# A list scheduler inside the kernel sets the order of a fused windowed attention and MLP-mixer on one core

## The chip, the core and the metric

The kernel runs on one core of a Trainium2 chip. The core has five engines that work side by side: TensorE (PE, matrix products), VectorE (DVE), ScalarE (ACT), GpSimd (POOL) and SyncE (SP, which here only issues transfers), and 16 DMA engines that move data. Each engine works through its own instructions strictly in the order in which the program lists them, and waits where an operand is not ready. The metric is the device time of one execution in microseconds (us); lower is better.

## What is computed

Four batches, eight heads, 768 positions, head size 64; all in float32 in memory. `n_sink` is 4 and `window` is 128.

```python
scores = scale * np.matmul(q, k.transpose(0, 1, 3, 2))      # (4, 8, 768, 768)
keep = is_sink | in_window                                  # first 4 keys, or 0 <= i-j < 128
a = softmax(np.where(keep, scores, -1e9))
x = (a @ v) laid out as (4, 768, 512)                       # heads side by side
h = np.maximum(x.T @ w_tok1, 0) @ w_tok2                    # token mixing, 768 -> 256 -> 768
u = x + h.T
out = u + np.maximum(u @ w_ch1, 0) @ w_ch2                  # channel mixing, 512 -> 1536 -> 512
```

## The kernel before

The work comes in eight groups of four heads (two groups to a batch) and four mixers (one to a batch). Tiles have 128 rows.

**Attention of a group.** q, k and v come as float32 and are cast to bf16 (`cast`, `cast_all` and `cast_v`, on POOL, DVE or ACT). q and k are turned so that the head dimension lies on the partitions: groups 0 to 3 by transposes on PE with a copy out of PSUM (`tr`), groups 4 to 7 by DMA transposes that SP issues (`turn`, line 126). `sc(j, u)` multiplies for one pair of heads `j` and a third `u` of the keys, in PSUM tile `ps_s`; ACT takes the exponential of all of it in one instruction (`pT`, line 252). In groups 0 and 1 the mask is added on PE (`mneg`, line 240), later it is applied to `pT` by POOL (lines 256, 263, 266). `sk` does the four sink keys (`ks`, `ps_k`, `pk`). `pv(qt)` multiplies with v (`va`) and `vsink` for a tile of 128 queries into `ps_o`, and DVE divides by the sum (lines 296 and 297) into `x_b`.

**Mixer of a batch.** `tok1` (tile `ps_h`, four pieces of six products), `tok2` (`ps_u`, six pieces of two; DVE adds `x_b` at line 340, which gives `u_sb`), `utr` (turns `u_sb` into `uT`: on PE for batch 0, by DMA for the others, line 344), `ch1` (`ps_v`, 24 pieces of four products 384 wide; a ReLU into `v`, on ACT at line 357 for even pieces and on DVE at line 359 for odd ones), `ch2` (`ps_w`, six tiles of 12 products 512 wide, in three parts of four; DVE adds `u_sb` at line 369, SP stores).

**PSUM.** Three pools of two tiles each: `ps_sc` for the scores (two banks to a tile), `ps_mx` for `ps_h`, `ps_v`, `ps_w` (and `ps_u` of batch 0), `ps_ms` for the rest.

**Order.** It is written out by hand. Attention and token mixing of batch 0 come first, as a list (`seq`). Then, for each batch `b`, the list `main` of its channel mixing is walked, and the list `fill` (attention and token mixing of batch `b + 1`, loads, casts) is put in at fixed shares of `main`'s cost by `spread`. Loads of q, k and v are one transfer of 768 KB for a group of heads (384 KB for the first ones). The line that places the late setup work of batch 0 is this one:

```python
fill += [(0.15, build_mask0), (0.2, lambda: cast_sinks(GB, NG))]
```

`build_mask0` is two writes by DVE (lines 173 and 180) with two selects by POOL (lines 174 and 177) between them; `cast_sinks` writes `vsink` on DVE (lines 195 and 198).

Of the kernel before, what the change touches and what calls it, by code (L numbers as in the profile page):

```python
# [1 line left out]

# [7 lines left out]
FP32 = mybir.dt.float32  # L10
BF16 = mybir.dt.bfloat16
AF = mybir.ActivationFunctionType
ALU = mybir.AluOpType


@with_exitstack
def kernel(
# [43 lines left out]
    ident = singles.tile([P, P], BF16, name="ident")  # L61
    mask0 = singles.tile([P, 2, 2, P], BF16, name="mask0")
    mneg = singles.tile([P, 2, 2, 2, P], BF16, name="mneg")
    warm = singles.tile([P, 512], BF16, name="warm")
    ks = [[singles.tile([P, P], BF16, name=f"ks{a}{j}") for j in range(2)] for a in range(2)]
    dm = singles.tile([4 * GH, GH, 1], FP32, name="dm")
    vs_c = singles.tile([4 * GH, NG, D], FP32, name="vs_c")
    vsink = singles.tile([P, NG, GH, D1], BF16, name="vsink")

    w_tok1 = singles.tile([P, NT, DTOK], BF16, name="w_tok1")  # L70
    w_tok2 = singles.tile([P, NTOK, S], BF16, name="w_tok2")
    w_ch1 = singles.tile([P, NC, DCH], BF16, name="w_ch1")
    w_ch2 = singles.tile([P, NF, DM], BF16, name="w_ch2")

    SYNC = mybir.DependencyInfo(mybir.DependencyClass.Sync, mybir.DependencyReason.DATA)

    def after(dma, *others):
        for o in others:
            tc.add_manual_dep(dma.ins, o.ins.name, SYNC, reason="order of loads")
        return dma  # L80

    class Group:
        pass

    def tiles(g):
        G = Group()
        G.b, G.h0 = g // GB, GH * (g % GB)
        G.dma = g >= 2 * GB
        G.q32 = stage.tile([P, GH, NT, D], FP32, name="q32")
        G.k32 = stage.tile([P, GH, NT, D], FP32, name="k32")  # L90
        G.qb = bfp.tile([P, 2, NT, 2, D], BF16, name="qb")
        G.kb = bfp.tile([P, 2, NT, 2, D], BF16, name="kb")
        G.v32 = stage.tile([P, GH, NT, D], FP32, name="v32")
        G.va = bfp.tile([P, GH, NT, D1], BF16, name="va")
        G.T, G.pT = [None, None], [None, None]
        return G


    def load_qk(eng, src, dst, G, lo, hi):
        return eng.dma_start(  # L100
            out=dst[:, lo:hi].rearrange("p h t d -> p h (t d)"),
            in_=src[G.b, G.h0 + lo:G.h0 + hi].rearrange("h (p t) d -> p h (t d)", t=NT)
        ) if not G.dma else eng.dma_start(
            out=dst.rearrange("p h t d -> p (h t) d"),
            in_=src[G.b, G.h0:G.h0 + GH].rearrange("h (t p) d -> p (h t) d", p=P))

    def load_q(G, lo, hi, eng=nc.sync):
        return load_qk(eng, q, G.q32, G, lo, hi)

    def load_k(G, lo, hi, eng=nc.sync):  # L110
        return load_qk(eng, k, G.k32, G, lo, hi)

    def cast(G, j, which, copy):
        src, dst = ((G.q32, G.qb), (G.k32, G.kb))[which]
        copy(dst[:, j].rearrange("p t i d -> p i t d"), src[:, 2 * j:2 * j + 2])

    def flat(G, which):
        return (G.qb, G.kb)[which].rearrange("p j t i d -> p (j t i d)")

    def cast_all(G, which, copy):  # L120
        copy(flat(G, which).rearrange("p (t h d) -> p t h d", t=NT, h=GH),
             (G.q32, G.k32)[which].rearrange("p h t d -> p t h d"))

    def turn(G, which):
        T = att.tile([P, 2 * NT, P], BF16, name="qT" if which == 0 else "kT")
        nc.sync.dma_start_transpose(out=T, in_=flat(G, which))
        G.T[which] = [T.rearrange("d (t j) p -> d t j p", j=2)[:, :, j] for j in range(2)]

    def by_dve(o, i):
        nc.vector.tensor_copy(out=o, in_=i)  # L130

    def by_pool(o, i):
        nc.gpsimd.tensor_copy(out=o, in_=i)

    def by_act(o, i):
        nc.scalar.activation(o, i, AF.Copy)
# [466 lines left out]
```

## Time and profile before

| | us |
|---|---|
| median of three runs | 231.0 (229.96 to 231.47) |
| span of the profiled execution, first to last instruction | 229.2 |
| PE busy in it | 205.5 (90%) |
| DVE, ACT, POOL busy | 107.0, 90.5, 93.9 |
| mean granted TensorE clock | 0.993 |

The profiled execution has its span as its own time; no other time was taken of it. Busy time of PE counts a product until its modelled end, so short pauses between products hide in it. "Busy" shares are a mean over stages that have different limits, so the stages are read one by one. In the chain of the work that ended last, a row is a start, a length and what ran; "issue" is time in which an engine waited for nothing that the profile shows. In the rows of an engine's timeline the brackets at the end give the pause before the first instruction of the row and what ended it.

### The profile page before, as it was taken

The page shows a single profiled execution, that of the slowest core. Times are in us where ns is not written, and L with a number is a line of the kernel's source. Part 1 is how long each engine was busy: PE and PEld are TensorE (multiplying, and loading weights), DVE is VectorE, ACT ScalarE, POOL GpSimd, SP SyncE. Part 2 cuts the span into 40 slices and gives each one's busy share as a digit, 9 for nine tenths or more (in the row PEclk, how much of TensorE's full clock was granted, in tenths as well). Part 3 has the DMA queues.
Part 4 walks back from the last instruction along what each step waited for, and adds up shares of the span by engine and source line. Part 5 has one row for each costly group of instructions (what it writes and reads, how often), then busy time and mean ns, then how long its engine had stood idle before and what let it go on. Part 6 is the DMA issues. An engine that isn't in the chain of part 4 may idle for free.

```text
span 229.2 us, 3886 instructions
## 1 busy us (share of the span) xinstructions
PE 205.5 (90%) x1547; PEld 111.3 (49%) x1565; DVE 107.0 (47%) x241; ACT 90.5 (40%) x152; POOL 93.9 (41%) x123
## 2 busy tenths in 40 slices
PE   7898868499799999788899999987999999999993
PEld 2444734255355654344466644444566444554441
DVE  5674635826375547222364464324337463333331
ACT  2798144027976210287752200777542001311100
POOL 8659732501878991057397700266640000000000
PEclk9999999979999999999999999999999999999999
DMA  6999999999879934869999738790001055001122
GB/s 208 342 228 155 211 306 232 296 269 214 166 148 217 229 99 108 169 171 213 218 220 207 167 82 164 170 186 0 24 25 46 3 160 160 0 0 49 46 92 92
DMA packets 76353, 34.88 MB, mean 152 GB/s; under 512 B 66400, under 2 KB 72288, under 8 KB 76336
## 3 DMA queue, kind: packets, MB, share of 16 engines
q1 hardware_dynamic: 70384, 24.65, 50.4%
q0 software_dynamic: 4992, 8.69, 17.1%
q10 hardware_dynamic: 960, 1.31, 1.7%
q8 instruction: 12, 0.20, 0.4%
q14 instruction: 5, 0.04, 0.1%
HBM read 26.77 MB, written 6.29 MB: 144 GB/s over the span
## 4 chain that ended last, share of the span: by engine, by line
PE 58%; DMA 13%; ACT 11%; DVE 7%; issue 5%; POOL 3%; SPq 1%; POOLq 0%; DVEq 0%
PE ps_w L366 26%; PE ps_v L354 18%; ACT pT L252 7%; DMA w_ch<-in_moe_w_ch_dram 5%; DMA v<-in_v_dram 5%; PE ps_h L332 3%; PE ps_u L339 3%; PE ps_s L246 2%; ACT v L357 2%; DVE o L369 2%; DMA k<-in_k_dram 2%; DMA kT<-kb 2%; PE ps_o L284 2%; PE ps_o L288 1%; PE ps_o L279 1%
## 5 line engine op out<-in xcount | busy, mean ns | idle before, releaser
L354 PE MATMUL ps_v<-uT,w_ch 128*128 128x384 bf16 x384 | 75.4, 331 | 7.4 <-ACT v L357 3.0
L366 PE MATMUL ps_w<-w_ch,v 128*128 128x512 bf16 x275 | 68.0, 379 | 2.7 <-ACT v L357 1.9
L357 ACT ACTIVATE v<-ps_v 128x384 bf16<-128x384 f32 x48 | 23.8, 495 | 81.7 <-PE ps_v L354 44.9
L354 PEld LDWEIGHTS <-w_ch 128*128 128x128 bf16 x384 | 35.9, 99 | 37.7 <-issue 17.8
L359 DVE TENSOR_SCALAR v<-ps_v 128x384 bf16<-128x384 f32 x48 | 26.6, 554 | 45.9 <-PE ps_v L354 45.9
L252 ACT ACTIVATE pT<-ps_s 128x1024 bf16<-128x1024 f32 (+1 forms) x48 | 43.6, 959 | 9.0 <-PE ps_s L246 8.7
L366 PEld LDWEIGHTS <-v 128*128 128x128 bf16 x288 | 27.1, 98 | 32.2 <-issue 4.2
L256 POOL TENSOR_TENSOR pT<-pT,mask 128x512 bf16<-128x512 bf16 x12 | 13.8, 1153 | 47.0 <-ACT pT L252 47.0
L369 DVE TENSOR_TENSOR o<-ps_w,u_sb 128x512 f32<-128x512 f32 x24 | 16.6, 692 | 18.7 <-PE ps_w L366 18.6
L340 DVE TENSOR_TENSOR u_sb<-ps_u,x_b 128x512 bf16<-128x512 f32 x24 | 16.2, 688 | 19.3 <-PE ps_u L339 19.1
L263 POOL TENSOR_SCALAR_AFFINE_SELECT pT<-pT 128x640 bf16<-128x640 bf16 x24 | 18.3, 761 | 11.0 <-ACT pT L252 11.0
L297 DVE TENSOR_TENSOR x_b<-ps_o,rc 128x256 bf16<-128x256 f32 x42 | 17.8, 424 | 1.4
L296 DVE RECIPROCAL rc<-ps_o 128x4 f32<-128x4 f32 x42 | 7.4, 177 | 22.6 <-PE ps_o L288 12.2
L246 PE MATMUL ps_s<-qT,kT 64*128 64x256 bf16 x192 | 15.4, 264 | 2.9 <-DMA kT<-kb 1.2
L284 PE MATMUL ps_o<-va,pT 128*128 128x65 bf16 x192 | 16.4, 194 | 0.0
L284 PEld LDWEIGHTS <-pT 128*128 128x128 bf16 x192 | 14.1, 98 | 3.0 <-issue 0.4
L266 POOL TENSOR_SCALAR_AFFINE_SELECT pT<-pT 128x512 bf16<-128x512 bf16 x24 | 15.5, 647 | 0.0
L288 PE MATMUL ps_o<-va,pT 128*128 128x65 bf16 x160 | 14.9, 194 | 0.0
L332 PE MATMUL ps_h<-x_b,w_tok 128*128 128x256 bf16 x96 | 13.4, 272 | 1.0 <-DVE x_b L297 0.5
L339 PE MATMUL ps_u<-h,w_tok 128*128 128x512 bf16 x46 | 13.5, 379 | 0.7 <-DVE u_sb L340 0.3
L246 PEld LDWEIGHTS <-kT 64*128 64x128 bf16 x192 | 6.8, 94 | 14.1 <-issue 9.4
L334 ACT ACTIVATE h<-ps_h 128x256 bf16<-128x256 f32 x16 | 6.1, 383 | 18.8 <-PE ps_h L332 18.8
(63 smaller groups left out, 173.1 us busy)
## 6 DMA issues: line engine op xcount, KB each, us to landing
out_dram<-o SPq DMA_DIRECT2D x23, 256.0 KB, 2.2
v<-in_v_dram SPq DMA_DIRECT2D x6, 768.0 KB, 10.0
w_ch<-in_moe_w_ch_dram POOLq DMA_DIRECT2D x4, 768.0 KB, 14.1
q<-in_q_dram SPq DMA_DIRECT2D x4, 768.0 KB, 8.6
k<-in_k_dram SPq DMA_DIRECT2D x4, 768.0 KB, 10.4
q<-in_q_dram SPq DMA_DIRECT2D x4, 384.0 KB, 6.9
q<-in_q_dram POOLq DMA_DIRECT2D x2, 768.0 KB, 16.9
k<-in_k_dram POOLq DMA_DIRECT2D x2, 768.0 KB, 18.4
```

The costliest lines, as they stand in the source:

```text
L246: nc.tensor.matmul(ps[:, i, at:at + w].rearrange("p (c q) -> p c q", q=P), G.T[1][j][ds(64 * i, 64), kt], G.T[0][j][ds(64 * i, 64), kt:kt ...
L252: nc.scalar.activation(pT[:, :, 512 * u:512 * u + n], ps[:, :, 0:n], AF.Exp, scale=scale)
L263: nc.gpsimd.affine_select(out=cur, in_=cur, compare_op=ALU.is_ge, fill=0.0, base=0, pattern=[[0, NT - 1], [1, P]], channel_multiplier=-1)
L284: nc.tensor.matmul(o, pT[:, i, ds(256 * qt, P)], G.va[:, h, qt], start=(qt < 2 and h == 0), stop=(h == GH - 1 and qt == 0), skip_group_che ...
L297: nc.vector.tensor_tensor(out=x_b[:, qt, c0:c0 + GH * D].rearrange("p (h d) -> p h d", h=GH), in0=o[:, :, 0:D], in1=rc.to_broadcast([P, GH ...
L332: nc.tensor.matmul(ps, w_tok1[:, t, ts(tt, P)], x_b[:, t, ds(a * GH * D, GH * D)], start=(t == 0), stop=(t == NT - 1))
L339: nc.tensor.matmul(ps, w_tok2[:, tt, ts(st, P)], h1[:, tt], start=(tt == 0), stop=(tt == NTOK - 1))
L354: nc.tensor.matmul(ps, w_ch1[:, c, ts(ft, P)], uT[:, c, ds(half * HS, HS)], start=(c == 0), stop=(c == NC - 1))
L357: nc.scalar.activation(v1[:, ft, ds(half * HS, HS)], ps, AF.Relu)
L359: nc.vector.tensor_scalar(out=v1[:, ft, ds(half * HS, HS)], in0=ps, scalar1=0.0, scalar2=None, op0=ALU.max)
L366: nc.tensor.matmul(ps, v1[:, ft, ts(st, P)], w_ch2[:, ft], start=(ft == 0), stop=(ft == NF - 1))
L369: nc.vector.tensor_tensor(out=o, in0=ps, in1=u_sb[:, st], op=ALU.add)
```

## The change

All tiles are static (one allocation each, two or four copies with letters, `qTa`, `qTb`). The work is described as a list of tasks, each with engines that may run it, a duration, the tasks that it needs and a priority. A list scheduler (`Plan.order`) walks a clock and starts, on each free engine, the ready task with the lowest priority number; the tasks are then emitted in the order in which they started. The durations are formulas in the code; the hardware sees nothing of them but the order.

```diff
+class Plan:
+    LAT = {"PE": PE_TAIL + SEM, "ACT": 0.115 + SEM, "DVE": 0.093 + SEM, "POOL": 0.05 + SEM, "SP": 0.05}
...
+            for e in engines:
+                if free[e] > now + 1e-9:
+                    continue
...
+                    if len(t.eng) > 1:
+                        ends = {x: max(free[x], now) + self.cost(t, x) for x in t.eng}
+                        best = min(ends.values())
+                        if ends[e] > best + 0.12:
+                            held.append(item)
+                            continue
+                    if t.need:
+                        got = pick(t.need, now)
...
+def pe(*cols):
+    return sum(c / 2400 + 0.0025 for c in cols)
...
-    ps_sc = ctx.enter_context(tc.tile_pool(name="ps_sc", bufs=2, space=bass.MemoryType.PSUM))
-    ps_mx = ctx.enter_context(tc.tile_pool(name="ps_mx", bufs=2, space=bass.MemoryType.PSUM))
-    ps_ms = ctx.enter_context(tc.tile_pool(name="ps_ms", bufs=2, space=bass.MemoryType.PSUM))
+    ps_s = [psp.tile([P, 2, 512], FP32, name=f"ps_s{x}") for x in "ab"]
+    ps_g = [psp.tile([P, 512], FP32, name=f"ps_g{x}") for x in "abcd"]
...
+    CH = {"load": 0, "tr": 6, "sc": 7, "sk": 5, "pv": 4, "tok1": 3, "tok2": 2, "ut": 1}
...
+    l_ch1 = [load("POOL", w_ch1[:, :, ts(i, c1)], moe_w_ch1.rearrange("(t p) n -> p t n", p=P)[:, :, ts(i, c1)], 3.1,
+                  gate, prio=next(pp)) for i in range(N1)]
...
+        if G.dma:
+            for n, (src, dst, ld) in enumerate(((q, q32, "lq"), (k, k32, "lk"))):
+                setattr(G, ld, [load("SP", dst[s][:, h], rows_in_tiles(src, g, h, h + 1)[:, 0], 1.1, [*after_cast, *hold_back(b)],
+                                     prio=b * 10 + 8 + (g % GB), hold=0.95) for h in range(GH)])
...
+        size = 1 if g == 0 else 2
+        for n in range(0, 6, size):
+            todo = units[n:n + size]
...
+            m = add("PE", cost, f, [*[G.T[w][j] for w in range(2) for j in need], *([t_mneg] if first else [])],
+                    prio=pr(g, "sc"), need=("s", len(todo)), slot=slots)
...
+            M.v[half, ft] = add(("ACT", "DVE"), either(HS), e, [m, *(old.ch2[3 * half:3 * half + 3] if old else [])],
+                                prio=5, slot=slot, frees=True)
...
+                if b == B - 1 and st == NT - 1:
+                    ch2(st, 0, 256, False)
+                    ch2(st, 256, 128, False)
+                    ch2(st, 384, 128, True)
```

What this does to the program, part by part:

- **Four one-bank PSUM tiles** `ps_ga` to `ps_gd` serve everything but the scores, in any order; the two score tiles `ps_sa`, `ps_sb` stay. Scores after group 0 come in bursts of two units that take both score tiles at once.
- **Copies, ReLUs and casts** go to ACT or DVE (casts of the early groups also to POOL), whichever the plan sees free first.
- **The masks, the sink tiles and their writes** are made in the first microseconds.
- **Loads.** `w_ch1` comes in three pieces of 512 columns, `w_ch2` in two, all before q, k and v of group 2; v of groups 0 and 1 is issued by POOL and no longer by SP. q, k and v of groups 4 to 7 come one head at a time (192 KB).
- **POOL's masks** of groups 2 to 7 come in two pieces per pair of heads, the first after two of the three exponentials; before, they all came after the third.
- **The last output tile** is computed and stored in pieces of 256, 128 and 128 columns.

The instructions on PE are otherwise the same: 24 `ch1` pieces and six `ch2` tiles to a batch.

On DVE, around the first ReLUs of batch 0's channel mixing, the order before was (`u_sb` is the add of token mixing, `v_112` a ReLU):

```order
L340 TENSOR_TENSOR u_sb<-ps_u,x_b 128x512 x4
L359 TENSOR_SCALAR v_112<-ps_v 128x384
L340 TENSOR_TENSOR u_sb<-ps_u,x_b 128x512 x2
L173 MEMSET mask_92 128x512
L180 MEMSET mask_92 4x512
L359 TENSOR_SCALAR v_112<-ps_v 128x384
L195 TENSOR_SCALAR vsink<-vs_c,dm 16x6x64
L198 CAST vsink<-dm 16x6
```

In the change those writes of the mask stand among the first casts of the program (`kba` and `qba` are k and q of group 0 in bf16):

```order
L296 MEMSET mneg 4x128
L276 CAST kba<-k32a 128x2x6x64
L405 MEMSET mask_62 128x512
L276 CAST qba<-q32a 128x2x6x64
L407 MEMSET mask_62 4x512
L276 COPY qTa<-ps_gb 128x768
```

The mask has moved from between two ReLUs to the program's start, ahead of the copy of group 0's first turned q.

On ACT, at the start of batch 1's channel mixing, where group 4's attention begins, the order before was (`pT` an exponential of scores, `v_572` a ReLU of `ch1`, `ks` small copies of sink keys):

```order
L357 ACTIVATE v_572<-ps_v 128x384 x2
L229 ACTIVATE ks_95<-kT 64x4 x2
L229 ACTIVATE ks_96<-kT 64x4 x2
L252 ACTIVATE pT<-ps_s 128x2x512 x2
L357 ACTIVATE v_572<-ps_v 128x384
L252 ACTIVATE pT<-ps_s 128x2x384
L252 ACTIVATE pT<-ps_s 128x2x512
L357 ACTIVATE v_572<-ps_v 128x384 x2
```

In the change it is this (`v_110` is the ReLU):

```order
L274 ACTIVATE ksxb<-kTa 64x4 x2
L561 ACTIVATE pTa<-ps_sa 128x2x512
L604 ACTIVATE pka<-ps_gc 128x512
L561 ACTIVATE pTa<-ps_sb 128x2x512
L561 ACTIVATE pTa<-ps_sa 128x2x384
L561 ACTIVATE pTb<-ps_sb 128x2x512
L561 ACTIVATE pTb<-ps_sa 128x2x512
L561 ACTIVATE pTb<-ps_sb 128x2x384
L721 ACTIVATE v_110<-ps_gb 128x384
```

All six exponentials of group 4 now stand before the first ReLU of this batch; on PE the three bursts of scores that they read stand before its first `ch1` piece, with only the two sink products between the first burst and the second.

On SP, where the loads of groups 6 and 7 are issued, the order before was (`uT` and `qT`, `kT` are DMA transposes):

```order
L126 DMA_TRANSPOSE qT<-qb 128x12x128
L126 DMA_TRANSPOSE kT<-kb 128x12x128
L103 DMA q_1342<-in_q_dram 128x24x64
L103 DMA k_1343<-in_k_dram 128x24x64
L139 DMA v_1346<-in_v_dram 128x24x64
L103 DMA q_1351<-in_q_dram 128x24x64
L103 DMA k_1352<-in_k_dram 128x24x64
L139 DMA v_1355<-in_v_dram 128x24x64
```

In the change, from the transposes of batch 1 on:

```order
L702 DMA_TRANSPOSE uTb<-u_sbb 128x4x128 x5
L484 DMA_TRANSPOSE qTb<-qbb 128x12x128
L319 DMA k32b<-in_k_dram 128x6x64 x2
L319 DMA v32b<-in_v_dram 128x6x64 x4
L319 DMA q32a<-in_q_dram 128x6x64 x3
L484 DMA_TRANSPOSE kTb<-kbb 128x12x128
L319 DMA q32a<-in_q_dram 128x6x64
L319 DMA k32a<-in_k_dram 128x6x64 x4
L319 DMA v32a<-in_v_dram 128x6x64 x4
```

Each load has become four, and transposes stand between them: `kTb` waits in SP's order behind nine of the small loads.

More of the change, by code (lines that the diff above doesn't have):

```diff
@@ L72 @@
[L72 to L96, printed above, removed]
@@ new lines, in flat, with on, copy, zero @@
+    def flat(slot):
+        p, b = slot.at
+        return ps_g[b] if p == "g" else ps_s[b][:, 0]
+    plan = Plan({"s": [0, 1], "g": [0, 1, 2, 3]})
+    add = plan.add
+    def on(t):
+        return {"ACT": nc.scalar, "DVE": nc.vector, "POOL": nc.gpsimd}[t.on]
+    def copy(t, o, i):
+        if t.on == "ACT":
+            nc.scalar.activation(o, i, AF.Copy)
+        else:
+            on(t).tensor_copy(out=o, in_=i)
+    def zero(tile_, eng="DVE", n=512):
+        return add(eng, n * 0.00104, lambda t: on(t).memset(tile_, 0.0), prio=0)
@@ L195, in cast_sinks, with f @@
+    t_dm = add("POOL", 0.4, build_dm, prio=20)
+    z_vs = add("DVE", 1.9, lambda t: nc.vector.memset(vsink, 0.0), prio=30)
+    def cast_sinks(lo, hi, h):
+        def f(t):
             nc.vector.tensor_scalar(
```

954 lines of the change are left out of this document (561 added, 393 removed).

## The prediction

> **What bounds the kernel now.** The page comes first, then the busy time of the engines by stage, then the chain and the timelines of those stages.
>
> ```profile
> PE 205.5 (90%) x1547; PEld 111.3 (49%) x1565; DVE 107.0 (47%) x241; ACT 90.5 (40%) x152; POOL 93.9 (41%) x123
> ...
> PE   7898868499799999788899999987999999999993
> ...
> PEclk9999999979999999999999999999999999999999
> DMA  6999999999879934869999738790001055001122
> ```
>
> PE is busy for 90% of the span, and no other engine for half of it, so PE's own work and PE's pauses make the time. The dip to 7 in the clock row and the nines in the first ten DMA slices are used below. In the next view a row is a stage, its length, busy time (and count) of PE, its weight loads, DVE, ACT and POOL, granted clock, DMA share, GB/s. I cut the span at PE's starts: its first transpose (5.92), the restart after a pause (44.63), the first `ch1` of batches 1, 2 and 3, and the last product's end.
>
> ```profile
> 5.92:44.63 38.71, 30.89 (x308) 17.26 (x311) 23.88 (x63) 21.01 (x31) 23.19 (x32) 1.00 1.15 248
> 44.63:93.32 48.69, 45.68 (x367) 25.77 (x372) 25.64 (x58) 21.29 (x32) 27.06 (x32) 0.96 0.86 184
> 93.32:142.81 49.49, 45.75 (x349) 25.24 (x352) 21.39 (x48) 20.33 (x38) 23.81 (x28) 1.00 0.93 180
> 142.81:191.55 48.74, 45.97 (x349) 25.33 (x352) 21.40 (x48) 20.26 (x38) 15.04 (x20) 1.00 0.34 83
> 191.55:225.25 33.70, 33.11 (x167) 16.25 (x167) 10.83 (x18) 5.88 (x12) 0.00 (x0) 1.00 0.16 55
> 225.25:229.20 3.95, 0.00 (x0) 0.00 (x0) 0.69 (x1) 0.00 (x0) 0.00 (x0) 1.00 0.19 66
> ```
>
> Busy time hides short pauses, so I compare each stage with its work, counted from what one piece takes when nothing holds PE up:
>
> ```profile
> 66.08 0.34 PE ps_tr L215 x6
> ...
> 115.47 0.49 PE ps_s L246 x8
> ...
> 118.81 0.43 PE ps_k L273 x2
> 119.24 0.65 PE ps_v L354 x4
> 119.89 0.65 PE ps_h L332 x6
> ...
> 122.22 0.86 PE ps_w L366 x4
> ...
> 137.80 0.43 PE ps_u L339 x2
> ```
>
> From these, six transposes take 0.34, a burst of eight score products 0.49, sink keys 0.43, a `ch1` piece 0.65, a `tok1` piece 0.66, a `ch2` part 0.86, a `tok2` piece 0.43. The rest comes from starts in PE's timeline:
>
> ```profile
> 8.41 0.59 PE L240 MATMUL ps_s<-mneg,ident 128*128 128x512 bf16 x2
> 8.94 0.39 PE L246 MATMUL ps_s<-qT,kT 64*128 64x256 bf16 x4
> 9.27 0.51 PE L215 MATMUL ps_tr<-ident,kb 128*128 128x128 bf16 x6
> ...
> 70.45 0.27 PE L279 MATMUL ps_o<-vsink,pk 128*128 128x260 bf16 x1
> ...
> 70.81 0.28 PE L279 MATMUL ps_o<-vsink,pk 128*128 128x260 bf16 x1
> ```
>
> Mask products take 0.53 a unit (8.41 to 8.94), four scores alone 0.33 (8.94 to 9.27), a `pv` tile with sinks 0.36 (70.45 to 70.81).
>
> A batch's channel mixing is 24 x 0.65 + 18 x 0.86 = 31.1 us. Attention and token mixing of a later batch are 6 x 0.49 + 2 x 0.43 + 2 x 1.84 + 4 x 0.66 + 6 x 0.43 = 12.7 (a group's six `pv` tiles: four of 0.36, one of 0.25, one of 0.15, the latter two by their numbers of products). Batch 1 has eight sets of transposes more: 15.4. Batch 0 costs 23.6 before its channel mixing: the 12.7 without bursts (9.8), 12 units of mask and lone scores (8 x 0.86 + 4 narrow ones x 0.70 = 9.7), 8 sets of transposes (2.7) and those of `u_sb` (1.4). The total is 188.8 us of 229.2. The other 40.4 are pauses:
>
> - start, to 5.92: 5.9
> - B, 5.92 to 44.63: 38.7 less 23.6 and the seven `ch1` pieces that PE's timeline has between 33.24 and the restart (4.6): 10.5
> - C, 44.63 to 93.32: 48.7 less 15.4 and 26.5 of channel mixing: 6.8
> - D, 93.32 to 142.81: 49.5 - (31.1 + 12.7) = 5.7
> - E, 142.81 to 191.55: 48.7 - 43.8 = 4.9
> - F, 191.55 to 225.25: 33.7 - 31.1 = 2.6
> - tail after PE's end: 4.0
>
> The change leaves PE's work as it is, up to 24 products of 128 columns and 12 of 256 in place of 12 of 512 for the last tile; at a sixth of the 0.34 and half of a quarter of the 0.86 that is 2.7 for 2.6. What it is worth is decided by these seven pauses.
>
> **Stage B.** ACT paces attention of batch 0, then the late setup stops everything:
>
> ```profile
> 5.43 0.84 ACT L136 ACTIVATE kb<-k 128x768 bf16<-128x768 f32 x1 [1.76 <-DMA k<-in_k_dram]
> ...
> 8.18 1.02 ACT L252 ACTIVATE pT<-ps_s 128x1024 bf16<-128x1024 f32 x1 [0.49 <-PE ps_s L246]
> ...
> 22.08 0.81 ACT L252 ACTIVATE pT<-ps_s 128x768 bf16<-128x768 f32 x1
> ```
>
> ```profile
> 8.18 0.83 POOL L133 CAST kb<-k 128x768 bf16<-128x768 f32 x1 [0.28 <-DMA k<-in_k_dram]
> ```
>
> ```profile
> 33.62 1.42 POOL L139 DMA_DIRECT2D v<-in_v_dram  x1 [3.41 <-DMA w_ch<-in_moe_w_ch_dram]
> 39.05 0.41 POOL L174 TENSOR_SCALAR_AFFINE_SELECT mask<-mask 128x256 bf16<-128x256 bf16 x1 [4.02 <-DVE mask L173]
> ```
>
> ```profile
> 44.63 5.67 PE L354 MATMUL ps_v<-uT,w_ch 128*128 128x384 bf16 x23 [2.89 <-DVE v L359]
> ```
>
> POOL was free at 35 and waited 4.02 us for DVE's first write of the mask, which stands in DVE's order behind the adds; DVE then waits for POOL's two selects, writes the mask again, and after one ReLU writes `vsink` eight times before the next, on which PE waits 2.89 us at 44.63. The seven pieces before it are 4.6 us, so it is as if the channel mixing had started unbroken at 40.1. The change takes this stop out: the mask stands in the first microseconds, where it costs DVE two writes that wait for POOL (some 1 us before the first copy of q).
>
> It also gives ACT more to do there: two casts more (0.84 each, its row at 5.43) and three pairs of sink copies (0.4 a pair by their 0.2 each), together 2.9. Its first exponential, at 8.18 before, now stands behind the cast of the second k, whose data came at 8.18 by POOL's row, a copy of 0.81 and two sink copies: 10.8. The exponentials ended at 22.9; with 2.9 more work and a pause of about 1 us in each paired burst (the next one starts only when both tiles are free) I take 27, between 25.8 (work alone) and 29. What follows it is a chain through DVE:
>
> ```profile
> L297 DVE TENSOR_TENSOR x_b<-ps_o,rc 128x256 bf16<-128x256 f32 x42 | 17.8, 424 | 1.4
> ```
>
> Three divisions (0.42 and a reciprocal before each, 0.6) to 29.3 with the `pv` tile and its hand-over, two `tok1` pieces 1.3, a ReLU and hand-over 0.6, a `tok2` piece and three adds of 0.69 to 33.8, a transpose and its copy 1.2: first `ch1` at about 35, and with the transposes and `tok2` pieces still between, an unbroken start at 36.4. The gain is 40.1 - 36.4 = **3.7**, between 1.7 (exponentials at 29) and 5.
>
> **Stage C.** The granted clock is 0.96 over 48.7 us, which is a loss of 1.9, and the page's dip stands right behind the pause at 44.63; without the pause I count it gone. [...]
>
> Of the remaining 4.9 most are waits for a ReLU behind exponentials on ACT, or for a cast. Four banks let PE run two `ch1` pieces further ahead, and the ReLU goes to the freer engine. I take 1.8 off those; C gains **3.7**, between 6.8 (no pause left) and a loss of 4 if group 2's data are late (first rival).
>
> **Stages D and E.** Here the waits can be named:
>
> ```profile
> 96.94 0.61 PE L246 MATMUL ps_s<-qT,kT 64*128 64x256 bf16 x8 [1.21 <-DMA kT<-kb]
> ...
> 102.24 1.46 PE L354 MATMUL ps_v<-uT,w_ch 128*128 128x384 bf16 x8 [0.58 <-ACT v L357]
> ...
> 111.41 1.02 PE L366 MATMUL ps_w<-w_ch,v 128*128 128x512 bf16 x3 [0.97 <-ACT v L357]
> ```
>
> 1.21 us for kT's DMA transpose, then three waits, of which the first (0.58) and the last (0.97) are shown, for ReLUs that ACT ran only after two exponentials; together 3.4. The other 2.3 of D are short. kT of group 4 is now issued before batch 0's last store, so the first wait goes; ReLUs on either engine and four banks take most of the others. What is late next: at D's start all three bursts of group 4 stand together with little between them, and each waits for about two exponentials; and uT's first transpose stands behind four loads on SP. I count 2.5 for this and 1.0 for the rest: D falls from 5.7 to 3.5, **2.2**, between 0 and 4.5. In E two or three `ch2` parts stand between the bursts: 4.9 to 2.2, **2.7**, between 0.5 and 4.5.
>
> **Stage F and tail.** With two banks a `ch1` piece waits for the ReLU of the piece two before; 24 of them and three crossings into `ch2` stand in the 2.6. With four banks I leave 0.6: **2.0**, between 1 and 2.6. At the end:
>
> ```profile
> 225.25 0.69 DVE o L369
> ```
>
> The add of 512 columns takes 0.69, the division's 256 columns took 0.42, so 128 take nearer 0.25: **0.4**, between 0 and 0.5; the stores' landing stays.
>
> **Loads.** The transfers of the late weights took long from issue to landing:
>
> ```profile
> w_ch<-in_moe_w_ch_dram POOLq DMA_DIRECT2D x4, 768.0 KB, 14.1
> ```
>
> Loads fill the first 57 us (DMA digits 9 to slice ten), and the bytes are the same, so the order decides. `w_ch1` had landed when POOL's row at 33.62 was released from its wait for that transfer; it still comes behind the same first loads, and is needed at 35. After it eight transfers took until about 57 us, some 3.0 each; the two of `w_ch2` now go first, so q of group 2 lands near 42, k 45, v 48, q of group 3 at 51, k at 54. PE needs them after 17 `ch1` pieces and on: q near 47.5, k near 50, group 3's near 55.6 and 57.7. The cover is 3 to 5 us, less a cast. I cost it at nothing.
>
> v of group 0 goes the other way. Before, its wait and landing were a link of the chain:
>
> ```profile
> 5.43 10.63 DMA v<-in_v_dram
> ```
>
> POOL now issues it behind the mask's selects, which wait for DVE's first cast near 5.4, so near 7.1; with the same 10.6 and a cast it is there near 19.5, about when the first `pv` comes. Nothing is charged; each us later would be one in B.
>
> For the split loads of groups 4 to 7, the rows of SP's queue.
>
> ```profile
> 63.83 0.37 SPq L103 DMA_DIRECT2D q<-in_q_dram  x1
> ...
> 108.07 3.43 SPq L139 DMA_DIRECT2D v<-in_v_dram  x1
> ...
> 138.07 1.23 SPq L344 DMA_TRANSPOSE uT<-u_sb  x1
> 139.40 1.43 SPq L126 DMA_TRANSPOSE qT<-qb  x1
> ```
>
> An issue that nothing holds takes 0.37, one of 768 KB that pushes through 3.43. A quarter of 3.43 is 0.86, taken; the bounds are 0.37 and the whole 3.43 (a cost that does not shrink with size). 48 loads at 0.86, 8 qT and kT at 1.43, 18 uT at 1.23 and some 17 stores at the 0.37 too are 81 us of the 122 us between the first store (near 70) and 191.55: SP keeps up. POOL's masks in more pieces have their finer start in return; POOL is busy 27.1 of 48.7 us at most, so nothing is charged.
>
> **Sum.** 3.7 + 3.7 + 2.2 + 2.7 + 2.0 + 0.4 = 14.7; 229.2 - 14.7 = 214.5 for the profiled execution. The median of the runs, 231.0, stood 1.8 above that span: **216.3**.
>
> **Rivals.**
>
> 1. *Data late in C.* PE's order is fixed, so each us beyond the cover of 3 to 5 is a us of PE. For it: the landing time of 14.1 us above, and v now on POOL's queue too. Against: equal bytes. At 4 to 8 us lost: 220 to 224.
> 2. *The pauses only move* (the change does not do what it says). 18 bursts after stage B need both score tiles; if each waits 0.8 (two exponentials of 1.02 against PE's work between the bursts), that is 14.4: 231. Against: two or more `ch2` parts or transposes stand between most of them.
> 3. *SP becomes the bound; slower.* 81 - 41 = 40 us go to other issues, so SP is full at 82 / 48 = 1.7 us a load. From there each 0.1 us costs 4.8 us, and at 2.0 the gain is gone; at 2.3 it is 245. Against: 0.37 and 0.86. [...]
> [...]
>
> **Chances.** Forecast 0.70, late data 0.13, pauses moved 0.08, clock 0.04, SP 0.05. With all gains at their upper bounds together (23.9) the forecast ends at 207, with all at their lower ones (C at 1.8, as with a new dip; 5.0 in all) at 226. Range: 208 to 227; it takes in the first and fourth rivals and leaves out the second and third, 0.13. Within 1% (228.7 to 233.3) is about what a measurement of this kernel cannot tell from no change: 0.06, the most of rival 2. Faster by more 0.89, slower by more 0.05.
>
> **What would show it.** Right: no pause of PE over 1 us between its first `ch1` and the end but at D's start, the clock at 1.00 after the start, first `ch1` near 35, F near 31.7, kT never the releaser of a score. Wrong: PE released by casts of q or k in C, score products released by exponentials all along, SP's own queue without pauses through D, or exponentials of batch 0 ending after 29.

## The result, and the profile after

The changed kernel took 215.5 us (median of four runs, 214.0 to 216.7) against 231.0 (229.96 to 231.47): a ratio of 0.933, with an interval of 0.927 to 0.939. The forecast was 216.3. Its profiled execution took 216.5, with a span of 214.8. Three kernels tried below have a profiled execution that took longer than their median (ReLUs fixed, 221.4; sink copies on ACT alone, 217.9; all three edits, 218.5), so the sizes of their waits are an indication only. The page of the changed kernel, where the lines of PE and of its clock answer to those of before:

```profile
PE 202.9 (94%) x1587; PEld 114.5 (53%) x1587; DVE 93.0 (43%) x221; ACT 107.7 (50%) x187; POOL 95.8 (45%) x163
...
PEclk9979999999999999769999999999999999999999
```

The dip behind 41 us is gone, and two new ones stand at slices 3 and 17 to 18 (of 40, 5.4 us each). By stage (cut at the first transpose, `ch1`'s unbroken start at 37.99, group 4's scores at 85.10, batch 3's first `ch1` at 180.53 and the last product), with the two slow stretches below; columns as in the prediction:

```profile
5.98:37.99 32.01, 27.69 (x285) 16.20 (x285) 26.58 (x64) 19.65 (x31) 18.64 (x21) 0.95 1.18 247
37.99:85.10 47.11, 47.07 (x400) 27.50 (x398) 22.12 (x51) 28.66 (x52) 27.71 (x47) 1.00 0.89 206
85.10:180.53 95.43, 92.06 (x705) 51.50 (x705) 35.67 (x90) 46.34 (x80) 47.22 (x84) 0.96 0.74 145
180.53:211.73 31.20, 31.20 (x193) 17.77 (x191) 4.59 (x9) 11.78 (x24) 0.00 (x0) 1.00 0.14 51
211.73:214.80 3.07, 0.17 (x3) 0.00 (x0) 0.50 (x2) 0.00 (x0) 0.00 (x0) 1.00 0.52 171
9.90:13.30 3.40, 3.40 (x24) 1.73 (x24) 3.06 (x3) 2.60 (x5) 3.40 (x4) 0.51 1.10 286
88.40:95.20 6.80, 5.64 (x27) 2.59 (x25) 0.61 (x2) 3.90 (x7) 6.80 (x15) 0.51 0.66 124
```

Less the prediction's work (23.6 and one `ch1` piece in B; 15.4 and 30.4 in C; twice 43.8; 31.1), the pauses are these. The column of "four tiles" is an experiment told below, counted in the same way.

| stage | before | forecast | changed | before with four tiles |
|---|---|---|---|---|
| start | 5.9 | 5.9 | 6.0 | 5.9 |
| B | 10.5 | 6.8 | 7.8 | 5.6 |
| C | 6.8 | 3.1 | 1.3 | 5.2 |
| D and E | 10.6 | 5.7 | 7.8 | 4.4 |
| F | 2.6 | 0.6 | 0.1 | 0.2 |
| tail | 4.0 | 3.6 | 3.1 | 4.0 |
| sum | 40.4 | 25.7 | 26.0 | 25.3 |

The sum came out as forecast, its terms did not. In PE's timeline of the changed kernel, D's head shows where most of the 7.8 lie:

```profile
8.97 0.51 PE L494 MATMUL ps_gc<-ident,kba 128*128 128x128 bf16 x6 [1.53 <-ACT kba L274]
...
36.58 0.81 PE L740 MATMUL ps_ga<-uTa,w_ch 128*128 128x384 bf16 x4
37.99 0.81 PE L740 MATMUL ps_ga<-uTa,w_ch 128*128 128x384 bf16 x4
...
86.67 0.34 PE L543 MATMUL ps_sa<-qTa,kTa 64*128 64x256 bf16 x4 [0.42 <-ACT pTa L561]
88.07 0.40 PE L543 MATMUL ps_sb<-qTa,kTa 64*128 64x256 bf16 x4 [1.06 <-ACT pTa L561]
88.78 0.61 PE L543 MATMUL ps_sa<-qTa,kTa 64*128 64x256 bf16 x4 [0.31 <-ACT pTa L561]
89.69 0.51 PE L543 MATMUL ps_sb<-qTa,kTa 64*128 64x256 bf16 x4 [0.31 <-ACT pTb L561]
...
146.08 0.39 PE L543 MATMUL ps_sa<-qTb,kTb 64*128 64x256 bf16 x4 [0.72 <-DMA kTb<-kbb]
```

Four waits for exponentials (2.1 in all) with nothing between the bursts, and 6.8 us at a clock of 0.51 that begin beside the last two of them (88.40). E has no wait over 0.16 but the 0.72 for kT. The wait of 1.53 at 8.97 likewise stands ahead of 3.4 us at 0.51 (9.90:13.30).

### The profile page after: what moved, and what is told of

Its sections match the earlier page's. It is cut to its first block, busy times and chain, and to the rows that moved or that the text cites. A ratio compares the mean times of both kernels' runs of the same rounds, so it can differ in the third digit from the quotient of the medians.

```text
span 214.8 us, 4152 instructions
## 1 busy us (share of the span) xinstructions
PE 202.9 (94%) x1587; PEld 114.5 (53%) x1587; DVE 93.0 (43%) x221; ACT 107.7 (50%) x187; POOL 95.8 (45%) x163
## 4 chain that ended last, share of the span: by engine, by line
PE 68%; DVE 8%; POOL 7%; issue 6%; DMA 5%; SPq 3%; ACT 1%; DVEq 0%; POOLq 0%
PE ps_gc L740 8%; PE ps_ga L759 8%; PE ps_gb L759 8%; PE ps_ga L740 7%; PE ps_gd L740 6%; PE ps_gb L740 6%; PE ps_gc L759 4%; PE ps_gd L759 3%; DMA kTb<-kbb 2%; PE ps_ga L825 2%; SPq L319 2%; PE ps_sa L543 2%; DVE u_sba L695 2%; DMA v32a<-in_v_dram 2%; DVE x_ba L647 1%
## 5 line engine op out<-in xcount | busy, mean ns | idle before, releaser
L740 PEld LDWEIGHTS <-w_ch 128*128 128x128 bf16 x384 | 37.3, 100 | 26.3 <-issue 2.5
L759 PE MATMUL ps_gb<-w_ch,v 128*128 128x512 bf16 (+1 forms) x96 | 23.4, 366 | 0.0
L759 PE MATMUL ps_ga<-w_ch,v 128*128 128x512 bf16 (+1 forms) x96 | 22.7, 359 | 0.0
L721 ACT ACTIVATE v<-ps_gb 128x384 bf16<-128x384 f32 x23 | 11.3, 491 | 19.4 <-PE ps_gb L740 16.4
L759 PE MATMUL ps_gc<-w_ch,v 128*128 128x512 bf16 x72 | 18.5, 379 | 0.0
L721 ACT ACTIVATE v<-ps_gd 128x384 bf16<-128x384 f32 x23 | 11.3, 491 | 10.9 <-PE ps_gd L740 10.6
L721 ACT ACTIVATE v<-ps_ga 128x384 bf16<-128x384 f32 x21 | 10.3, 491 | 10.2 <-PE ps_ga L740 10.2
L740 PE MATMUL ps_gb<-uTb,w_ch 128*128 128x384 bf16 x52 | 11.4, 346 | 0.0
L740 PE MATMUL ps_gd<-uTa,w_ch 128*128 128x384 bf16 x56 | 11.4, 326 | 0.0
L740 PE MATMUL ps_gc<-uTb,w_ch 128*128 128x384 bf16 x52 | 11.2, 341 | 0.0
L740 PE MATMUL ps_ga<-uTb,w_ch 128*128 128x384 bf16 x48 | 10.4, 343 | 0.0
L759 PE MATMUL ps_gd<-w_ch,v 128*128 128x512 bf16 (+1 forms) x48 | 10.4, 339 | 0.0
```

The costliest lines, as they stand in the source:

```text
L721: nc.scalar.activation(o, i, AF.Relu)
L740: nc.tensor.matmul(flat(slot)[:, 0:HS], w_ch1[:, c, ts(ft, P)], uT_[:, c, ds(half * HS, HS)], start=(c == 0), stop=(c == NC - 1))
L759: nc.tensor.matmul(flat(slot)[:, 0:cw], v1[:, ft, ts(st, P)], w_ch2[:, ft, ds(c0, cw)], start=(ft == 0), stop=(ft == NF - 1))
```

## Experiments

The theory was that PE's pauses went because of the four shared tiles, the freer engine for ReLUs and the setup writes moved out of DVE's way, and that D's loss is its head. The rivals: one part does it all; the order of issue does it and the tiles don't matter; the pauses only move.

**Four tiles in the kernel before.**

```diff
-    ps_mx = ...tile_pool(name="ps_mx", bufs=2, space=PSUM)
-    ps_ms = ...tile_pool(name="ps_ms", bufs=2, space=PSUM)
+    ps_mx = ...tile_pool(name="ps_mx", bufs=4, space=PSUM)
+    ps_ms = ps_mx        # and tag="mx" for every one-bank tile
```

> The kernel before, with its two pools of two one-bank PSUM tiles made one pool of four, used in turn; the written order of issue is unchanged. Theory (two more pieces of slack for PE in every stage of channel mixing): F's pause falls from 2.6 to under 1, D and E lose 1 to 2 each, 225 to 228 us. Rival (used in turn and not by choice, a tile held for three ch2 parts stops the others): 230 us or more.

Measured: **216.6 us, 0.937 (0.933 to 0.941)**. This one edit, in the old order, with the late setup, fixed ReLUs and whole loads, is worth as much as the whole change (216.6 in its own repeat below). Theory and rival both fell short of it. Its stages, cut at 37.70 (unbroken `ch1`, four pieces done), the first `ch1` of batches 1 to 3 and the last product:

```profile
5.92:37.70 31.78, 28.67 (x298) 15.80 (x299) 18.79 (x52) 19.67 (x28) 19.18 (x26) 1.00 1.15 248
37.70:86.80 49.10, 46.16 (x388) 26.48 (x385) 30.02 (x70) 22.92 (x35) 31.04 (x38) 1.00 1.03 218
86.80:133.52 46.72, 44.78 (x353) 25.23 (x352) 21.33 (x48) 20.26 (x38) 23.86 (x28) 1.00 0.99 191
133.52:178.80 45.28, 44.82 (x354) 25.23 (x353) 21.33 (x48) 20.26 (x38) 15.04 (x20) 1.00 0.34 83
178.80:210.10 31.30, 31.30 (x169) 16.33 (x167) 10.83 (x18) 5.88 (x12) 0.00 (x0) 1.00 0.20 67
```

The clock is 1.00 in all of them. DVE's late writes stand where they stood, and PE's waits beside them have shrunk from 2.89 to 0.58, now for ACT (rows of DVE, then of PE):

```profile
39.78 0.77 DVE L195 TENSOR_SCALAR vsink<-vs_c,dm 16x384 bf16<-16x384 f32 x1
...
43.01 1.47 DVE L359 TENSOR_SCALAR v<-ps_v 128x384 bf16<-128x384 f32 x3
```

```profile
41.78 1.46 PE L354 MATMUL ps_v<-uT,w_ch 128*128 128x384 bf16 x8 [0.58 <-ACT v L357]
43.82 2.11 PE L354 MATMUL ps_v<-uT,w_ch 128*128 128x384 bf16 x12 [0.58 <-ACT v L357]
```

With two more tiles PE goes on while three ReLUs wait on DVE (x3 at 43.01). What looked like a stop by the setup was a lack of tiles to work into.

**The split back in the changed kernel.**

```diff
-    plan = Plan({"s": [0, 1], "g": [0, 1, 2, 3]})
+    plan = Plan({"s": [0, 1], "g": [0, 1], "m": [2, 3]})
-            pools = ["s"] if cls == "s" else ["g", "s"] if not scores else ["g"]
+            pools = [cls]      # tok1, ch1, ch2, batch 0's tok2 need "m"
```

> The changed kernel with its four one-bank PSUM tiles split two and two as before (two for tok1, ch1, ch2 and batch 0's tok2, two for the rest), and planned anew for them; the last stage may not use the idle score tiles either. Theory (the free choice among four banks is what fills PE's pauses): the last batch's channel mixing (stage F) gets its pause of 2.6 us back, where the changed kernel has none, and C to E together gain 2 to 5 us of pauses; 219 to 224 us. Rival (the order of issue does it, banks hardly matter): F within 0.5 us of the changed kernel's 31.2, total 215 to 217.

Measured: 223.2, 0.965 (0.960 to 0.969), the theory's time. F and the tail are

```profile
185.11:218.95 33.84, 33.06 (x193) 17.66 (x191) 4.52 (x8) 11.78 (x24) 0.00 (x0) 1.00 0.15 54
218.95:222.00 3.05, 0.15 (x3) 0.00 (x0) 0.48 (x2) 0.00 (x0) 0.00 (x0) 1.00 0.30 92
```

so F's pause is 33.8 - 31.1 = 2.7 again, as the theory had it. The rest fell otherwise: of the 7.2 us between the two profiled spans (222.0 and 214.8), F has 2.6, C to E together only 1.4 (41.13 to 185.11, for 37.99 to 180.53), where 2 to 5 were expected, and B has 3.1 (`ch1` runs on from 41.13 for 37.99), which the theory did not name. The new order with split tiles is worth 8.0 us (231.2 to 223.2), the tiles in the old order 14.6, both together 14.6: they take away the same pauses, so their gains don't add.

**The setup alone**, moved early in the kernel before.

```diff
+        build_mask0()                          # behind build_sinks(), in the setup
-                    fill += [(0.15, build_mask0), (0.2, lambda: cast_sinks(GB, NG))]
-        seq += [lambda: cast_sinks(0, GB), C(G1, 1, 0, by_pool), ...
+        seq += [lambda: cast_sinks(0, GB), end_mask0, lambda: cast_sinks(GB, NG), C(G1, 1, 0, by_pool), ...
```

> The kernel before, with one thing changed: the mask's first write and its two selects stand in the first setup, its last write and the eight writes of vsink for batches 1 to 3 right behind those for batch 0, instead of behind 15 and 20% of batch 0's channel mixing. Theory (that stop was 2.9 us of PE's wait at 44.63 and 1.9 of a slow clock behind it): the stop and the dip are gone, 225 to 228 us. Rival (DVE's writes only move: they now hold up the divisions of batch 0, or PE waits next for the late data of group 2): 229 to 231.

Measured: 229.3, 0.991 (0.988 to 0.994), the rival's time. PE's timeline:

```profile
6.46 0.51 PE L217 MATMUL ps_tr<-ident,qb 128*128 128x128 bf16 x6 [1.36 <-POOL dm L187]
...
20.62 0.40 PE L248 MATMUL ps_s<-qT,kT 64*128 64x256 bf16 x4 [2.15 <-DVE qT L130]
...
42.09 7.30 PE L356 MATMUL ps_v<-uT,w_ch 128*128 128x384 bf16 x40
```

```profile
20.00:26.00 6.00, 5.29 (x56) 2.74 (x56) 2.72 (x10) 3.20 (x4) 6.00 (x8) 0.72 1.15 180
```

The stop is gone, but the first transposes start 0.54 later (6.46 for 5.92). The row names POOL's `dm`, which they don't read; DVE's cast of q, which they do, now ends at 6.40, since the mask's write stands ahead of it. The copy of qT stands behind DVE's other writes (2.15), and behind that wait the clock is 0.72 over 6 us (second fence, by stretch). Four `ch1` pieces (2.6) stand ahead of 42.09, so it is as if `ch1` had started unbroken at 39.5, for 40.1: 0.6 gained in B, where the prediction counted 3.7 with this as the ground. Another 1.3 came in C, which has a clock of 1.00 here (42.09:91.54). The place that I gave the writes cost waits of its own, so this run alone doesn't say what the stop was worth; the one with four tiles, where the writes stay late, does.

**ReLUs fixed again in the changed kernel.**

```diff
-                M.relu.append(add(("ACT", "DVE"), either(GH * D), e, ...
+                M.relu.append(add("ACT", act(GH * D), e, ...
-            M.v[half, ft] = add(("ACT", "DVE"), either(HS), e, ...
+            M.v[half, ft] = add(("ACT", "DVE")[ft % 2], either(HS)[("ACT", "DVE")[ft % 2]], e, ...
```

> The changed kernel, with the engine of each ReLU fixed as before (tok1's on ACT, ch1's on ACT and DVE by turns), planned anew; the four banks stay. Theory (ReLUs on the freer engine took the waits behind exponentials away): 2 to 4 us more in C to E, 218 to 221 us. Rival (four banks alone cover a ReLU that comes one or two exponentials late): within 1 us of the changed kernel, 215.5 to 217.5.

Measured: 219.5, 0.948 (0.944 to 0.953): 2.9 slower, the theory's, yet by another wait. None of PE's waits over 0.26 in C to E is for a ReLU. The longest are for sink copies that the new plan gave to DVE, and the rest those of D's head:

```profile
64.03 0.39 PE L598 MATMUL ps_gb<-qTb,ksyb 128*128 128x512 bf16 x1 [1.91 <-DVE ksyb L276]
...
91.69 0.49 PE L598 MATMUL ps_gb<-qTa,ksxb 128*128 128x512 bf16 x1 [1.92 <-DVE ksxb L276]
```

The old order with four tiles has fixed ReLUs too and reaches 216.6, so what they cost depends on the plan around them; that ReLUs on the freer engine gain by themselves isn't shown.

**The clock.** The changed kernel once more, then with products whose result is never read, put where PE idles: at D's head, and at 7.5 us.

> The changed kernel once more, to be timed beside the others. Every theory: 214 to 217 us, 0.93 of the kernel before; the mean granted clock 0.976 or 0.99, as in its four runs so far.

> The changed kernel with eight 128x512 products of zeros (and two tiny ones) put where PE waits for exponentials at D's head: two before the third unit of scores, four before the fourth, one each before the fifth and sixth; their result is never read. Theory (the half-clock window of 6.8 us there is brought on by PE's four short pauses, 2.1 us in all): no such window in D, ch1 pieces there take 0.65 again instead of 1.25, 3.4 us less, 211 to 213.5, mean clock 0.99. Rival (the window has another cause): it stays, ch1 pieces at 1.25, 215 to 217.

```diff
+        fillers = {(0, 2): 2, (1, 0): 4, (1, 1): 1, (1, 2): 1} if g == 4 else {}
...
                 for (j, u), slot in zip(todo, slots):
+                    for _ in range(fillers.get((j, u), 0)):
+                        nc.tensor.matmul(flat(wslot), warm[:, 0:P], warm, start=True, stop=True)
```

> The changed kernel with five 128x512 products of zeros after its second set of transposes, where PE idles 1.53 us near 7.5 (the kernel before has single such products at these places, the changed one none); their result is never read. Theory (the idle time brings on the half-clock window at 10 to 13 us, but ACT's exponentials, the first of them at 10.8, pace batch 0): the window is gone or later, first exponential still at 10.8, at most 0.7 us gained, 215.5 to 217. Rival (PE's products pace it there too): 1.7 us gained, 214.5 to 215.3. Third (the window has another cause): it stays.

```diff
+            if g == 0 and w == 0 and j == 0:
+                add("PE", 0.21 * 5, lambda t: [nc.tensor.matmul(flat(wslot), warm[:, 0:P], warm, ...) for _ in range(5)],
+                    [m], prio=-1, need=("g", 1), slot=wslot, frees=True)
```

Measured: the repeat 216.6 (0.936, 0.933 to 0.940); filled at the head 215.1 (0.929, 0.925 to 0.934); filled at the start 214.6 (0.929, 0.925 to 0.933). The same stretches of the repeat, of the one filled at the head, and of the one filled at the start:

```profile
94.00:97.40 3.40, 3.40 (x28) 2.18 (x26) 1.67 (x6) 0.98 (x2) 2.68 (x7) 0.59 1.25 134
```

```profile
94.00:97.40 3.40, 3.40 (x46) 2.45 (x45) 1.64 (x7) 1.83 (x4) 2.60 (x7) 1.00 1.08 216
```

```profile
9.90:13.30 3.40, 2.88 (x33) 1.54 (x31) 3.16 (x5) 2.93 (x4) 3.40 (x4) 1.00 1.10 287
```

Each filled place has a clock of 1.00. The start's is worth 2.0 us against the repeat, which was timed apart from it, and 0.8 against the first four runs. The rival's time came, and my theory that the exponentials hide the slow stretch fell. The first exponential is at 10.16 for 10.80, the last ends at 28.02 for 29.62, and `ch1` starts unbroken at 36.39 less one piece, 35.7 for 37.3:

```profile
10.16 1.02 ACT L565 ACTIVATE pTa<-ps_sa 128x1024 bf16<-128x1024 f32 x1
...
27.21 0.81 ACT L565 ACTIVATE pTd<-ps_sb 128x768 bf16<-128x768 f32 x1
```

```profile
36.39 0.81 PE L744 MATMUL ps_gc<-uTa,w_ch 128*128 128x384 bf16 x4
```

Not all of this is the clock, since the plan was made anew: a pair of sink copies (0.42) that stood on ACT ahead of the first exponential now runs on DVE. A cleaner comparison is the profile of the kernel with whole loads, told further below. Its batch 0 has the changed kernel's order on ACT, DVE and POOL, PE waits as long in the same place, and yet the clock stays at 1.00:

```profile
9.01 0.51 PE L494 MATMUL ps_gc<-ident,kba 128*128 128x128 bf16 x6 [1.43 <-ACT kba L274]
```

```profile
9.90:13.30 3.40, 3.24 (x35) 1.73 (x36) 3.06 (x6) 3.31 (x6) 3.40 (x4) 1.00 1.08 288
5.97:35.61 29.64, 25.95 (x282) 15.59 (x285) 23.79 (x64) 19.30 (x31) 19.00 (x21) 1.00 1.18 242
```

There the first exponential is at 10.84, the last ends at 27.25, and the stage takes 29.64 for 32.01: the slow stretch costs 2.4 us in batch 0. PE paces from the second exponential on, which starts at 11.76 there and waits for products at a clock of 0.51 in the changed kernel:

```profile
12.56 1.02 ACT L561 ACTIVATE pTa<-ps_sb 128x1024 bf16<-128x1024 f32 x1 [0.73 <-PE ps_sb L543]
```

So the stretch does not follow the idle time each time. In the eight profiles of the changed kernel and its variants in which this place is not filled, PE waits 1.43 to 1.56 there; seven have a clock of 0.51 to 0.65 in 9.90:13.30, this one 1.00. The two in which it is filled have 1.00.

The head's is worth 1.6, half of what was forecast, and the two intervals touch. In the repeat the slow stretch was 3.4 us long and came behind a wait that the first profile's slow clock had covered, for POOL's mask; that wait stays when the head is filled, and is followed by a clock of 1.00 there:

```profile
93.63 0.23 PE L627 MATMUL ps_gd<-vaa,pTb 128*128 128x65 bf16 x2 [2.04 <-POOL pTb L572]
```

```profile
93.56 0.23 PE L638 MATMUL ps_gc<-vaa,pTb 128*128 128x65 bf16 x2 [2.00 <-POOL pTb L583]
```

The repeat's waits at D's head are as long as those of the first profile, yet its slow stretch is half as long and begins later: 3.4 us (0.59 in 94.00:97.40, and still 1.00 in 88.40:91.80) for 6.8 (0.51 in 88.40:95.20). PE was idle for 1.53 us ahead of the stretch in batch 0 and for 2.1 in all ahead of the one at D's head. How much idle time is enough, and where, is not shown: with the start filled, waits of 2.3 at D's head are followed by a stretch of about 3.4 us (0.57 in 88.10:91.50).

**Work at D's head.** Useful work in place of zeros: group 4's scores unit by unit, batch 0's last `ch2` parts held back for it; then its sink copies on ACT alone.

```diff
-        size = 1 if g == 0 else 2
+        size = 1 if g in (0, 4) else 2
...
+        for p, t in enumerate(held_parts):     # ch2 parts of batch 0's last tile
+            t.deps.append(Gs[4].burst[p + 1])
```

> The changed kernel with useful work at D's head: group 4's scores go one unit at a time, and batch 0's last three ch2 parts are held back until the second, third and fourth unit. Theory (D's 6.4 us of loss are the waits for exponentials, 2.1, and the half clock after them, 3.4): waits under 0.3 us each, no half-clock window in D, 210 to 212.5. Rival (the ch2 parts were needed where they stood, since PE waits there for kT or for the adds ahead of tok2's copies): 2 to 2.6 us of new waits at 80 to 83 us, 213.5 to 217.

> The kernel with batch 0's last ch2 parts between group 4's single units of scores, and group 4's two sink copies on ACT alone, which is idle there for 2.1 us while DVE has six adds in its queue. Theory (the 2.12 us wait for a sink copy at 85.74 is what ate that version's gain): 212 to 214 us. Rival (the wait only moves on to the next thing that group 4 needs, the mask on POOL or the fourth uT): 214.5 to 216.5.

Measured: 216.1 (0.933, 0.929 to 0.937) and 217.1 (0.936, 0.931 to 0.942): no gain that can be told in either. The first has its rival's time, though the new wait is for a sink copy and not where the rival put it; the second lies above its rival's range. Rows of the first, then of the second:

```profile
85.74 0.39 PE L598 MATMUL ps_gc<-qTa,ksxb 128*128 128x512 bf16 x1 [2.12 <-DVE ksxb L276]
...
108.79 0.39 PE L543 MATMUL ps_sa<-qTb,kTb 64*128 64x256 bf16 x4 [0.79 <-DMA kTb<-kbb]
```

```profile
108.72 0.39 PE L543 MATMUL ps_sa<-qTb,kTb 64*128 64x256 bf16 x4 [2.10 <-DMA kTb<-kbb]
```

The sink copy's wait went as planned, and 20 us later PE waits longer for kT of group 5: these scores start at 108.7 or 108.8 either way.

**All three edits**: both fills, and group 4's `pv` tiles behind `ch1` pieces.

```diff
+        for qt, t in enumerate(Gs[4].pv):
+            t.deps.append(mixers[1].ch1[5 if qt == 0 else 6])
```

> The changed kernel with three edits together: the five products of zeros at 7.5 us (alone 2.0 us gained), the eight at D's head (alone 1.6), and group 4's pv tiles held back behind the sixth and seventh ch1 piece of batch 1, since the mask of pTb on POOL, on which the first of them waits 2.0 us at 93.6, is done only at 93.57. Theory (the first two are independent losses to the clock, the third a pause that the plan's order makes): 216.6 - 2.0 - 1.6 - 1.5 = 211.5, between 210.5 and 213 us, clock 1.00. Rival (D's loss only moves: token mixing of batch 2, now later, holds the stage's end): 213 us or more.

Measured: 216.0 (0.935, 0.932 to 0.939); the theory fell, and the rival's time came by another chain than it named. In its profile no wait for the mask is left, and kT ends two longer ones; behind the second the clock is 0.57 in 146.50:149.90. With SP's and POOL's rows ahead of the first:

```profile
92.55 1.43 SPq L484 DMA_TRANSPOSE qTb<-qbb  x1
94.03 1.53 SPq L319 DMA_DIRECT2D k32b<-in_k_dram  x2
...
101.08 3.86 SPq L484 DMA_TRANSPOSE kTb<-kbb  x1
```

```profile
98.41 1.46 POOL L276 CAST kbb<-k32b 128x1536 bf16<-128x1536 f32 x1 [3.01 <-DMA k32b<-in_k_dram]
```

```profile
107.16 0.39 PE L551 MATMUL ps_sa<-qTb,kTb 64*128 64x256 bf16 x4 [2.21 <-DMA kTb<-kbb]
...
146.36 0.39 PE L551 MATMUL ps_sa<-qTb,kTb 64*128 64x256 bf16 x4 [2.86 <-DMA kTb<-kbb]
```

Two loads of group 5's k stand on SP behind qT's transpose, POOL's cast waits 3.01 for them, and kT's transpose waits for the cast. With only the head filled the same scores started at 108.19 without a wait, for 109.88 in the repeat; what is saved at the head beyond that is given back here. I infer this from the rows; k's loads ahead of the transposes weren't tried.

**Whole loads** for groups 4 to 7.

```diff
-  [load("SP", dst[s][:, h], rows_in_tiles(src, g, h, h + 1)[:, 0], 1.1, ..., hold=0.95) for h in range(GH)]
+  [load("SP", dst[s].rearrange("p h t d -> p (h t) d"), heads(src, g, 0, GH)..., 4.4, ..., hold=3.4)]
```

> The changed kernel with one load of 768 KB for each of q, k and v of groups 4 to 7 instead of one per head (12 loads for 48), planned anew with 3.4 us of SP for each. Theory (these loads lie beside PE's work, whole or in pieces): 215.5 to 217.5 us, no stage's length off by more than 1 us. Rival (a whole load holds SP while the transposes of uT or kT wait, as 3.43 us of issue did before): D and E 1 to 2 us longer each, 218.5 us or more.

Measured: 217.4 (0.940, 0.934 to 0.945), beside the repeat's 216.6 (0.936, 0.933 to 0.940), timed apart from it: no difference in the total that can be told. The stages of its profile differ by more than the theory allowed. B is 2.4 us shorter, by the clock that this execution kept. D and E are 97.83 for 95.43, 2.4 longer, with waits as the rival had them, for uT and for kT:

```profile
82.71:180.54 97.83, 91.00 (x697) 51.09 (x705) 38.31 (x98) 43.45 (x74) 46.04 (x83) 0.98 0.74 143
```

```profile
89.64 1.44 PE L740 MATMUL ps_gb<-uTb,w_ch 128*128 128x384 bf16 x4 [1.31 <-DMA uTb<-u_sbb]
...
102.44 0.39 PE L543 MATMUL ps_sa<-qTb,kTb 64*128 64x256 bf16 x4 [0.96 <-DMA kTb<-kbb]
```

The plan is another one in D and E as well, so how much of this is the loads' is not shown. That the cut loads carry some of the gain stays open.

**Four tiles and two small edits** in the kernel before.

```diff
-                lo, mid = (0.36, 0.80) if b == 0 else (0.06, 0.68)
+                lo, mid = (0.36, 0.80) if b == 0 else (0.11, 0.68)
+            for c0, cw, eng in ((0, 256, nc.sync), (256, 128, nc.sync), (384, 128, nc.scalar)):   # last tile
```

> The kernel before with one pool of four one-bank PSUM tiles, and two small edits: the fills of batches 1 and 2's channel mixing begin at 11% of it instead of 6% (PE waits 1.56, 0.38 and 0.29 us for kT in the run with four banks), and the last tile of the last batch is computed, added and stored in 256, 128 and 128 columns as in the changed kernel (its tail is 3.1 us, that of the run with four banks 4.0). Theory (four banks carry the gain, and these two waits are what is left that an edit reaches): 216.6 - 1.9 - 0.9, or 213 to 214.5 us. Rival (the scores that come later make the masks, or token mixing at the stage's end, late): 215.5 us or more.

Measured: 215.1 (0.930, 0.926 to 0.934), between the two. kT's first wait (1.56) went, but the second grew from 0.38 to

```profile
100.78 0.61 PE L246 MATMUL ps_s<-qT,kT 64*128 64x256 bf16 x8 [1.26 <-DMA kT<-kb]
```

The lowest median of all is that of the changed kernel filled at the start (214.6), but it can't be told from this one (215.1) or from the head filled (215.1): their intervals overlap. All its six runs (214.2 to 215.5) lie under the repeat's six (216.1 to 217.2), though not under the first four of the changed kernel (214.0 to 216.7).

## Why the prediction was right, and where it was not

The total was right (216.3 for 215.5), and so was its ground: PE's work stays and the pauses decide. The terms were not: 1.0 and 2.1 too much was counted in B and in D and E, 1.8, 0.5 and 0.5 too little in C, F and the tail. That they cancel to 0.3 is luck. (The range, 208 to 227, stands 1 us above the two sums that it names, 207 and 226; nothing hangs on it.) Of the prediction's own signs, F came as said (31.2) and in this profile no pause over 1 us stands behind the first `ch1` but at D's start; the clock was not at 1.00 after the start, kT did release a score (0.72), and batch 0's exponentials ended after 29, which was a sign of being wrong.

- **B, 3.7 forecast, 2.7 measured** (37.3 for an unbroken start at 36.4). The first exponential came at 10.80 as worked out (the links named add to 10.2; the transposes between the cast and the copy make up the rest), the last ended at 29.6 for 27. The step that failed is the one that leaves the clock alone: in the new order PE idles for 1.53 us between the first transposes, where before a product of zeros and mask products followed, and the slow stretch behind that costs 2.4. Where it did not come, the exponentials ended at 27.25, as forecast. A second error hid part of this: from the last exponential to the unbroken start 9.4 us were counted, and it was 7.7 in both profiles. The cause was misplaced as well: the setup "stops everything" only where two tiles are left, and moved by itself it gained 0.6 of B.
- **C, 3.7 forecast, 5.5 measured.** The data came in time (first rival out), and the dip of 41 us went with the pause: the clock is 1.00 in 37.99:85.10. The 1.8 that the lower sum has for C, with a new dip, is shown by no run; in the changed kernel slow stretches came in B and at D's head, behind waits of 1.53 and of 2.1 in all.
- **D and E, 4.9 forecast, 2.8 measured.** The three bursts at the head were named and sized right (2.5 with a wait for uT that did not come; measured 2.1). Not counted were the half clock behind them, POOL's mask (0.55 here, 2.04 in the repeat), and kT of groups 5 and 7, which comes too late once more is saved ahead of it.
- **F 2.0, measured 2.5; tail 0.4, measured 0.9.** Both small and to the good; the column pieces did what the add's length had promised, and more.
- **Loads at nothing:** the total bears it out, and SP did not become the bound (third rival out): in its queue's rows the 48 loads take 36.5 us, 0.76 each, for the 1.7 at which it would be full. That the cut is free in D and E isn't shown: with whole loads they were longer. What matters, by the rows of all three edits, is which of SP's entries stand ahead of kT's.
- **Clock (0.04 of the chances):** in the changed kernel it was 1.00 in C and F; in D and E it was 0.51 in the 6.8 us that begin beside the waits at D's head, and 1.00 from 95.20 on (95.20:180.53).
- The chief error is in how the sum was made: gains of tiles, ReLUs, order and setup were laid side by side as if each took its own pauses. They stand in for one another, as 8.0, 14.6 and both at 14.6 show.

## What to carry to other kernels

Before an order is planned anew, share what the order has to wait for: two pools of two PSUM tiles made one pool of four were worth 14.6 us of 231 without another change. A wait that names an engine (DVE's ReLU behind setup writes, 2.89 us) may be a lack of buffers, and a trial with one pool (0.58) tells it apart from a slow engine. When a pause is filled, look for the next chain that reaches the same instruction: here exponentials, POOL's mask and kT's loads lay within 2 to 3 us of each other.

## What the hardware showed that was not expected

Pauses far shorter than the slow stretch were followed by about half clock: 1.43 to 1.56 us of idle time ahead of about 3.4 us in seven profiles (0.51 to 0.65 in 9.90:13.30), and four waits of 2.1 in all ahead of 6.8 (0.51 in 88.40:95.20). It is not certain to come: an eighth profile with 1.43 us idle in the same place kept its clock (1.00), and about the same waits at D's head were followed by 6.8 us in one, 3.4 in another, and in the repeat by none until a further wait of 2.04. Five products of zeros in the first place, in time that PE would have idled, gained 2.0 us against the repeat and 0.8 against the first four runs.
